# Last row of the output weights loaded and multiplied in two halves of 256 columns

## The chip, the core and the metric

One core of one Trainium2 chip runs the kernel. The metric is the device time of one execution in microseconds (us). The core has TensorE (matmuls and their weight loads), VectorE, ScalarE, GpSimd and SyncE, which work beside one another and wait for each other on semaphores, and 16 DMA engines that move data between the device memory and the on-chip memory. In profile lines they are PE (matmul) and PEld (weight load), DVE, ACT, POOL and SP; SPq and ACTq are DMA issues by SyncE and ScalarE. L38 is line 38 of the kernel, and since TensorE's instructions are written out by a helper there, all of them have that line.

## The reference

One decode step: a normalised row x (512 values) gives queries for 32 heads; each head attends to 8192 cached keys and values of 128; the heads' outputs go through `wo`. A gated unit on the same normalised row gives a gate, and the result is x plus the product of the two. All is float32.

```python
def _A_ref(x, k_cache, v_cache, wq, wo):          # H = 32, Dh = 128, D = 512
    q = (x @ wq) as [B, H, 1, Dh]
    scores = jnp.einsum("bhqd,bhkd->bhqk", q, k_cache) * (Dh ** -0.5)
    p = _softmax(scores, axis=-1)
    o = jnp.einsum("bhqk,bhkd->bhqd", p, v_cache)
    return o as [B, 1, H * Dh] @ wo               # wo: 4096 x 512

def _B_ref(x, w_gate, w_up, w_down):
    return (sigmoid(x @ w_gate) * (x @ w_up)) @ w_down

xn = _layernorm(x)
return x + _A_ref(xn, ...) * _silu(_B_ref(xn, ...))
```

(`_A_ref` and `_B_ref` are abridged here. The kernel takes the gate as the product of the unit's sum with its sigmoid.)

## The kernel before

**Stages.** Queries, gate and up weights come first. Then 16 pairs of heads are worked through (`NP`, the loop at line 440): VectorE multiplies a pair's keys with the query and sums them (`scores`), ScalarE takes the exponents (`powers_of`), TensorE multiplies them with the values (`pair`, 128 records of 512 columns for each pair), and the pair's output is turned into columns of `o_all` (`place`). All large loads are issued by SyncE in program order, each as soon as its slot is free. ScalarE issues the load of x at the start (line 240).

**The gate.** `column_sums` (line 327) puts the 512 sums of the gated unit onto four partitions, 0, 32, 64 and 96, with 128 consecutive columns each, and `g_row` holds sum times sigmoid in that layout (lines 370 to 373 and line 458). `x_row` holds x in the same layout.

**The tail.** `wo` is viewed as 128 partitions with 32 rows of 512 values each, row r of a partition following row r-1 in memory. It comes in nine loads that end at the rows in `W_ENDS` (line 91): rows 0 to 9, 10 to 15, and so on, at last rows 28 and 29 together, row 30 and row 31 (lines 483 to 485). A load of a single row has 128 runs of 2 KB. The first 28 rows (`W_FOLD`) are multiplied with their columns of `o_all` either on VectorE (`W_DVE`, lines 507 to 516) or on TensorE (`W_PE`, lines 521 to 525); `to_fold` adds these into `s_tmp`.

The rows 28 to 31 (`direct`, line 527) go straight into the sum `acc`, on the four partitions of the gate's layout: for each row four matmuls of 128 columns with one column of weights, one for each group of 32 columns of the array (lines 528 to 532). Behind row 30, `fold` adds the 128 partitions of `s_tmp` into the same `acc` with four matmuls whose weights are ones (lines 492 to 498). Row 31 is last. VectorE multiplies `acc` with `g_row` (line 537), adds `x_row` (line 539), and SyncE stores four runs of 512 bytes (line 562). Before that SyncE waits at line 552 for the load of row 30 (`ld_o[-2]`), goes through the branch at the end of the body, and then waits for the sum.

**What sets the order.** Nothing is planned: each engine follows its own program, and waits on semaphore counts. `Later` (line 18) notes TensorE's instructions and plays them in the order in which they were noted; the tail's are those in `after` (line 540).

Of the kernel before, what the change touches and what calls it, by code (L numbers as in the profile page):

```python
# [13 lines left out]
P = 128  # L14
# [37 lines left out]
def kernel(  # L52
# [13 lines left out]
    _, H, S, Dh = k_cache.shape  # L66
    D = x.shape[-1]
# [4 lines left out]
    NP = H // 2  # L72
    NG = 4
    GP = P // NG
    GC = D // NG
# [3 lines left out]
    WR = H * Dh // P  # L79
    WP = Dh // WR  # L80
# [10 lines left out]
    W_ENDS, W_FOLD = (10, 16, 20, 23, 26, 28, 30, 31, 32), 28  # L91
# [1 line left out]
    W_DVE = [r for r in range(W_FOLD) if r not in W_PE]  # L93
    V_CUTS, K_CUTS = (NB // 2, NB * 13 // 16), {NP - 3: (NB * 3 // 4,), NP - 2: (NB * 3 // 4,), NP - 1: (NB // 2,)}

    N_SEMS = 40
    DVE, ACT, SP, POOL = nc.vector, nc.scalar, nc.sync, nc.gpsimd
    PE = Later(nc.tensor)
    pe_only = OrderedEngineSet([nc.tensor.engine])
# [4 lines left out]
    s_out = nc.alloc_semaphore("s_out")  # L104

    def sb(name, *shape):
        return nc.alloc_sbuf_tensor(name, [P, *shape], F32)[:]
# [8 lines left out]

    pick = sb("pick", 2 * HT)
    slots = [sb(f"slot{i}", SLOT) for i in range(3)]
    x_row, g_row = sb("x_row", GC), sb("g_row", GC)
    ones, ident = sb("ones", P), sb("ident", P)  # L120


# [2 lines left out]
    s_tmp, part = q_all[:, :D], [q_all[:, (1 + n) * D:(2 + n) * D] for n in range(2)]  # L125
# [9 lines left out]
    o_all = sb("o_all", WR)  # L135
# [2 lines left out]
    psum = bank("psum", P, NK * QT)  # L138
    banks = [psum[:, i * QT:(i + 1) * QT] for i in range(NK)]
    big, po, wide = banks[:2], banks[2], banks[3:]  # L140
    acc, pt, o_t = wide[0][:, :GC], wide[1][:, :P], wide[2][:GP, :H * WP + Dh]
    pm, pn = wide[3][:, :4], wide[4][:GP, :Dh]


# [15 lines left out]
    pe, dve, act, pool = (Steps(n) for n in ("s_pe", "s_dve", "s_act", "s_pool"))  # L160
    loads = {}

    def load(eng, name, dst, src, *after):
        wait(eng, *after)
        if name not in loads:
            loads[name] = [semaphore(f"s_{name}"), 0]
        loads[name][1] += 16
        ins = eng.dma_start(dst, src)  # L168
        if not tc.compiled:
            tc.no_tile_sem_insts.add(ins.ins.name)  # L170
        ins.then_inc(loads[name][0], 16)
        return loads[name][0], loads[name][1]

    def wait(eng, *steps):
        for s in steps:
            if s is not None:
                eng.wait_ge(*s)
# [3 lines left out]
    maxed, reduced, powers, copied = (semaphore(f"s_{n}") for n in ("maxed", "reduced", "powers", "copied"))  # L181
# [6 lines left out]
    xv = x.rearrange("a b d -> (a b d)")  # L188
# [49 lines left out]

    c_xrow = dve(DVE.memset(x_row, 0.0))
    ld_xr = load(ACT, "xr", x_row[0:P:GP, :], xv.rearrange("(g c) -> g c", g=NG), c_xrow)  # L240
    ACT.nop().then_inc(q_free, NK)
    ACT.nop().then_inc(s_val[1], 16 * (NP - 2))
    ACT.nop().then_inc(s_val[2], 16 * (NP - 1))
# [17 lines left out]
    t = dve(DVE.reduce_sum(st[:, 0:1], x_col, axis=AX.X))  # L261
    wait(PE, t)
    t = pe(PE.matmul(pt[:, 0:1], ones, st[:, 0:1], start=True, stop=True))
    wait(DVE, t)
    t = dve(DVE.tensor_scalar(st[:, 1:2], pt[:, 0:1], 1.0 / D, None, op0=ALU.mult))
    wait(DVE, t)
    t = dve(DVE.tensor_scalar(xc, x_col, st[:, 1:2], None, op0=ALU.subtract))
    wait(DVE, t)
    t = dve(DVE.tensor_mul(sq, xc, xc))
    wait(DVE, t)  # L270
    t = dve(DVE.reduce_sum(st[:, 2:3], sq, axis=AX.X))
    wait(PE, t)
    t = pe(PE.matmul(pm[:, 0:1], ones, st[:, 2:3], start=True, stop=True))
    wait(ACT, t)
    t = act(ACT.activation(st[:, 3:4], pm[:, 0:1], AF.Sqrt, bias=eps_t, scale=1.0 / D))
    wait(DVE, t)
    t = dve(DVE.reciprocal(st[:, 4:5], st[:, 3:4]))
# [16 lines left out]
    for k in range(KT - 1):  # L294
        wait(DVE, ld_wq[k // 2] if k % 2 == 0 else None, t if k else None)
        t = in_place(wq_t, k)
# [5 lines left out]
              start=True, stop=True).then_inc(q_spread, 1)  # L302
    each_q = PE.take()
    for t in range(NQ):
        c = slice(t * QT, (t + 1) * QT)
        y = wq_t[:, 0, c]
# [3 lines left out]
        for e, h in enumerate(HALF):  # L310
            ins = ACT.copy(qb[h, 2 * t:2 * t + 2, :], q[h, :, e, :])
# [14 lines left out]

    def column_sums(dst, src):
        for g in range(NG):
            ins = PE.matmul(dst[g * GP:g * GP + 1, :GC], ones[:, 0:1], src[:, g * GC:(g + 1) * GC], start=True, stop=True)
        return pe(ins)  # L330

    rows = []
# [2 lines left out]
    for dst, src, ld in zip(sums, (wg_t, wu_t), (ld_g, ld_u)):  # L335
        wait(DVE, ld)
        for k in range(KT):
            t = in_place(src, k)
            wait(DVE, t)
        wait(PE, t, None if rows else (q_free, NK))  # L340
        for d, c in zip(dst, chunks):
            ins = PE.matmul(d[:, :c.stop - c.start], ones, src[:, 0, c], start=True, stop=True)
# [3 lines left out]
    for d, c in zip(sums[0], chunks):  # L346
        t = act(ACT.activation(sg[:, c], d[:, :c.stop - c.start], AF.Sigmoid))
    wait(DVE, t, rows[1])
    for d, c in zip(sums[1], chunks):
        t = dve(DVE.tensor_mul(hg[:, c], sg[:, c], d[:, :c.stop - c.start]))  # L350
# [3 lines left out]
    for g in range(NG):  # L354
        r = slice(g * GP, (g + 1) * GP)
        dve(DVE.transpose(hid[r, :FP, :], hg[r, g * FW:(g + 1) * FW].rearrange("p (i c) -> p c i", c=FP)))
    n = FL // NG
    for g in range(NG):
        r = slice(g * GP, (g + 1) * GP)
# [4 lines left out]
    for c in range(FP + FC):  # L364
        g = c % NG * GP
# [38 lines left out]
    summed, turned_out = {}, {}  # L404

    def all_max(i):
        DVE.wait_ge(turned, i + 1)
        DVE.reduce_max(mx[:1, 1:3], pt[0:1, :].rearrange("o (e p) -> o e p", e=2), axis=AX.X).then_inc(reduced, 1)  # L408
# [31 lines left out]
    for i in range(NP):  # L440
        if i > 0:
            all_max(i - 1)
        if i >= 2:
            load_keys(i, pieces(*K_CUTS.get(i, ())), summed[i - 2])
            if i < NP - 1:
                load_values(i - 1, FULL, (valued, i - 1))
        if i == NP - 1:
            for v, cut in ((i - 1, V_HALVES), (i, V_THREE)):
                load_values(v, cut[:1], (halved, v))
                load_values(v, cut[1:], (valued, v))  # L450
        scores(i)
        if i > 0:
            powers_of(i - 1)
            parts(i - 1)
            heads_out(i - 1)
        if i == 1:
            wait(DVE, c_sig)
            c_gate = dve(DVE.tensor_mul(g_row, g_row, big[1][:, :GC]))
    all_max(NP - 1)
    powers_of(NP - 1)  # L460
    wait(DVE, parts(NP - 1))
# [17 lines left out]


    wo_t = slots[NP % 2 ^ 1].rearrange("p (r e) -> p r e", e=D)
    ld_o = []
    for n, (r0, r1) in enumerate(zip((0,) + W_ENDS, W_ENDS)):
        ld_o.append(load(SP, f"wo{n}", wo_t[:, r0:r1, :], wo.rearrange("(p r) e -> p r e", r=WR)[:, r0:r1, :],
                         summed[NP - 2] if n == 0 else None))


    def to_fold(after):
        wait(DVE, after, t_part)
        return dve(DVE.tensor_add(s_tmp, part[0], big[0]))  # L490

    def fold(dst, copied, last):

        wait(PE, copied)
        for g in range(NG):
            ins = PE.matmul(dst[g * GP:g * GP + 1, :GC], ones[:, 0:1], s_tmp[:, g * GC:(g + 1) * GC],
                            start=last, stop=last)
        return ins

    piece = {r: ld for ld, *ends in zip(ld_o, (0,) + W_ENDS, W_ENDS) for r in range(*ends)}  # L500
# [6 lines left out]
    for k, r in enumerate(W_DVE):  # L507
        n = k % 2
# [16 lines left out]
                        start=(k < NG), stop=(k + NG >= len(W_PE)))  # L525
    folded = to_fold(pe(ins))
    direct = list(range(W_FOLD, WR))
    for r in direct:
        landed(PE, r, direct)
        for g in range(NG):  # L530
            ins = PE.matmul(acc[g * GP:g * GP + 1, :], o_all[:, r:r + 1], wo_t[:, r, g * GC:(g + 1) * GC],
                            start=(r == W_FOLD), stop=(r == WR - 1))
        if r == WR - 2:

            fold(acc, folded, False)
    wait(DVE, pe(ins))
    t = dve(DVE.tensor_mul(g_row, g_row, acc))  # L537
    wait(DVE, t)
    t = dve(DVE.tensor_add(g_row, g_row, x_row))  # L539
    after = PE.take()  # L540


# [6 lines left out]
        PE.play(each)  # L549
    PE.play(after)  # L550

    wait(SP, ld_o[-2])
    nc.regs_alu(once, once, 1, op=ALU.add)
    for e in (ACT, DVE, PE.engine, POOL, SP):
        br = e.br_lt(once, 1, on_true="body", on_false="leave")
# [3 lines left out]
    nc.switch_bb("leave")  # L559

    wait(SP, t)
    SP.dma_start(out.rearrange("a b (g c) -> (a b g) c", g=NG), g_row[0:P:GP, :]).then_inc(s_out, 16)


    used = sorted(s.num for s in sems)
# [33 lines left out]
```

## Time and profile before

| what | us |
|---|---|
| median of 3 runs | 684.65 |
| lowest and highest | 684.42, 684.74 |
| profiled execution | 684.69 |
| its span, first to last instruction | 683.3 |
| VectorE busy in it | 616.0 |
| TensorE matmuls busy in it | 218.8 |
| ScalarE busy in it | 44.6 |

The span is what the profile shows; 1.39 us of the profiled execution lie around it. All times in profile lines count from the span's start. A window line gives a stretch, its length, each engine's busy time with the number of instructions in flight, the clock granted to TensorE as a share of full speed, the busy share of the DMA engines, and GB/s. A timeline line gives start, duration, engine, line, operation, output<-inputs, shapes and count, and in brackets the engine's idle time before it and what ended that.

### The profile page before, as it was taken

The page shows a single profiled execution, that of the slowest core. Times are in us where ns is not written, and L with a number is a line of the kernel's source. Part 1 is how long each engine was busy: PE and PEld are TensorE (multiplying, and loading weights), DVE is VectorE, ACT ScalarE, POOL GpSimd, SP SyncE. Part 2 cuts the span into 40 slices and gives each one's busy share as a digit, 9 for nine tenths or more (in the row PEclk, how much of TensorE's full clock was granted, in tenths as well). Part 3 has the DMA queues.
Part 4 walks back from the last instruction along what each step waited for, and adds up shares of the span by engine and source line. Part 5 has one row for each costly group of instructions (what it writes and reads, how often), then busy time and mean ns, then how long its engine had stood idle before and what let it go on. Part 6 is the DMA issues. An engine that isn't in the chain of part 4 may idle for free. (4 is left out here: it accounts for less than half of the span.)

```text
span 683.3 us, 3400 instructions
## 1 busy us (share of the span) xinstructions
PE 218.8 (32%) x1376; PEld 62.3 (9%) x1376; DVE 616.0 (90%) x156; ACT 44.6 (7%) x142; POOL 2.6 (0%) x11
## 2 busy tenths in 40 slices
PE   0363025050503305050512306060512406060665
PEld 0120001010100101010100101010100101010110
DVE  3869999999999999998989899898989999999917
ACT  2040010000000100000010100000010101000010
POOL 0000000000000000000000000000000000000000
PEclk9987557575755757575665757575665757575897
DMA  9999999999999999999999999999999999999997
GB/s 382 429 440 460 437 434 430 430 430 430 430 430 430 430 430 430 460 441 445 434 430 430 430 430 430 430 430 430 430 437 437 460 430 403 472 399 430 435 430 331
DMA packets 7552, 293.67 MB, mean 430 GB/s; under 512 B 856, under 2 KB 864, under 8 KB 1664
## 3 DMA queue, kind: packets, MB, share of 16 engines
q1 hardware_dynamic: 7544, 293.67, 99.5%
q10 hardware_dynamic: 8, 0.00, 0.0%
HBM read 293.67 MB, written 0.00 MB: 430 GB/s over the span
## 5 line engine op out<-in xcount | busy, mean ns | idle before, releaser
L415 DVE TENSOR_TENSOR slot<-slot,q_all 128x16384 f32<-128x16384 f32 (+3 forms) x19 | 275.9, 14520 | 19.9 <-DMA slot<-in_A_k_cache_dram 19.9
L416 DVE TENSOR_REDUCE sc<-slot 128x128 f32<-128x16384 f32 (+3 forms) x19 | 276.0, 14525 | 0.7
L38 PE MATMUL psum<-slot,zeros 128*8 128x512 f32 x1024 | 148.5, 739 | 253.6 <-PEq L38 253.6
L38 PEld LDWEIGHTS psum<-slot,zeros 128*8 128x8 f32 x1024 | 30.3, 103 | 358.2 <-issue 358.2
L38 PE MATMUL psum<-ident,mx 128*1 128x128 f32 x32 | 8.4, 360 | 114.3 <-PEq L38 114.3
L437 ACT COPY o<-psum 128x512 f32<-128x512 f32 x16 | 9.4, 586 | 400.1 <-PE psum L38 400.1
L38 PE MATMUL psum<-slot,ones 128*128 (+3 forms) x36 | 17.7, 668 | 22.1 <-PEq L38 16.6
L290 DVE SCALAR_TENSOR_TENSOR slot<-slot,xn 128x1376 f32<-128x1376 f32 (+1 forms) x8 | 18.9, 2360 | 3.0 <-DMA slot<-in_A_wq_dram 2.7
L38 PE MATMUL psum<-o,pick 128*2 128x128 f32 x128 | 16.5, 272 | 12.8 <-PEq L38 12.8
L423 DVE STREAM_TRANSPOSE psum<-psum 32x128 f32<-32x128 f32 x16 | 5.0, 310 | 11.1 <-PE psum L38 11.1
L428 ACT ACTIVATE nb<-psum 128x2 f32<-128x2 f32 x16 | 2.8, 172 | 156.1 <-PE psum L38 156.1
L430 ACT ACTIVATE zeros<-sc,nb 64x128 f32<-64x128 f32 x32 | 12.8, 399 | 0.9
L38 PEld LDWEIGHTS psum<-ident,mx 128*1 128x1 f32 x32 | 1.8, 80 | 118.4 <-issue 118.3
L38 PEld LDWEIGHTS psum<-o,pick 128*2 128x2 f32 x128 | 9.9, 84 | 29.6 <-issue 27.2
L38 PE MATMUL psum<-slot,o_all 128*1 128x128 f32 (+1 forms) x54 | 9.5, 463 | 6.5 <-DMA slot<-in_A_wo_dram 6.5
L38 PE MATMUL psum<-zeros,rs 128*32 128x2 f32 x32 | 3.7, 187 | 23.5 <-PEq L38 23.5
L408 DVE TENSOR_REDUCE mx<-psum 1x2 f32<-1x128 f32 x16 | 4.4, 277 | 7.5 <-PE psum L38 7.5
L38 PE MATMUL psum<-mx,ones 1*128 1x2 f32 x32 | 8.2, 324 | 7.4 <-PEq L38 7.4
L515 DVE SCALAR_TENSOR_TENSOR q_all<-slot,o_all,q_all 128x512 f32<-128x512 f32 x15 | 10.0, 747 | 0.0
L38 PEld LDWEIGHTS psum<-slot,ones 128*128 128x128 f32 (+1 forms) x36 | 7.0, 218 | 32.5 <-issue 24.7
L38 PE MATMUL psum<-slot,o 128*1 128x512 f32 x26 | 5.0, 827 | 11.2 <-DMA slot<-in_B_w_down_dram 11.2
L38 PEld LDWEIGHTS psum<-mx,ones 1*128 1x128 f32 x32 | 7.3, 282 | 14.0 <-issue 14.0
(54 smaller groups left out, 61.3 us busy)
## 6 DMA issues: line engine op xcount, KB each, us to landing
slot<-in_A_k_cache_dram SPq DMA_DIRECT2D x2, 6144.0 KB, 37.9
slot<-in_A_v_cache_dram SPq DMA_DIRECT2D x3, 4096.0 KB, 23.0
slot<-in_A_wq_dram SPq DMA_DIRECT2D x2, 4096.0 KB, 16.6
slot<-in_A_k_cache_dram SPq DMA_DIRECT2D x2, 4096.0 KB, 40.5
slot<-in_A_k_cache_dram SPq DMA_DIRECT2D x2, 2048.0 KB, 42.4
slot<-in_B_w_gate_dram SPq DMA_DIRECT2D x1, 2752.0 KB, 26.9
slot<-in_B_w_up_dram SPq DMA_DIRECT2D x1, 2752.0 KB, 33.0
slot<-in_B_w_down_dram SPq DMA_DIRECT2D x1, 2560.0 KB, 22.7
```

The costliest lines, as they stand in the source:

```text
L38: ins = getattr(self.engine, name)(*args, **kwargs)
L290: return dve(DVE.scalar_tensor_tensor(y, w[:, k, cols], xn[:, k:k + 1], y, op0=ALU.mult, op1=ALU.add))
L408: DVE.reduce_max(mx[:1, 1:3], pt[0:1, :].rearrange("o (e p) -> o e p", e=2), axis=AX.X).then_inc(reduced, 1)
L415: wait(DVE, dve(DVE.tensor_mul(k[:, j, :], k[:, j, :], qb[:, i:i + 1, :].to_broadcast([P, n, Dh]))))
L416: summed[i] = dve(DVE.reduce_sum(sc[i % 2][:, j], k[:, j, :], axis=AX.X))
L423: turned_out[i] = dve(DVE.transpose(o, pn.rearrange("e (a r) -> e a r", r=WR)))
L428: wait(ACT, act(ACT.mul(nb, pm[:, :2], -SCALE)))
L430: ACT.activation(weights[h, :, e * HT:(e + 1) * HT], sc[i % 2][h].rearrange("p (g b) -> p g b", b=HT), AF.Exp, bias=nb[h, e:e + 1], scale= ...
L437: ACT.copy(o1, po).then_inc(copied, 1)
L515: ins = DVE.scalar_tensor_tensor(part[n], wo_t[:, r, :], col, part[n], op0=ALU.mult, op1=ALU.add)
```

## The change

The last row of `wo`, row 31, is loaded as two loads of 256 columns each (128 runs of 1 KB), so there are ten `wo` loads. The sum `acc` becomes two PSUM tiles of 64 columns in two banks, one for each half of the 512 columns; all matmuls that add into it, those of rows 28 to 30 and the fold too, are issued as eight of 64 columns instead of four of 128. When the first half of row 31 has landed, its four matmuls run and VectorE multiplies its 64 columns with the gate; then the same for the second half. One sum with x follows over all 128 columns.

The layout on the four partitions changes with it: each holds 64 columns of the first half and 64 of the second. So `column_sums` reads its operand with a stride, the store has eight runs of 256 bytes, and x is loaded a second time in the new layout into a new tile `x_add`, which is cleared at the start; ScalarE issues that load in the loop's second round, after the copy for pair 0. `x_row` stays for the normalisation. `N_SEMS` grows by two, and SyncE's wait before the branch names the load of row 30 as before, now `ld_o[-3]`.

```diff
-    x_row, g_row = sb("x_row", GC), sb("g_row", GC)
+    x_row, g_row, x_add = sb("x_row", GC), sb("g_row", GC), sb("x_add", GC)
...
-    acc, pt, o_t = wide[0][:, :GC], wide[1][:, :P], wide[2][:GP, :H * WP + Dh]
+    pt, o_t = wide[1][:, :P], wide[2][:GP, :H * WP + Dh]
+    acc = [wide[n][:, :GC // 2] for n in range(2)]
...
+    c_xadd = dve(DVE.memset(x_add, 0.0))
...
     def column_sums(dst, src):
         for g in range(NG):
-            ins = PE.matmul(dst[g * GP:g * GP + 1, :GC], ones[:, 0:1], src[:, g * GC:(g + 1) * GC], start=True, stop=True)
+            ins = PE.matmul(dst[g * GP:g * GP + 1, :GC].rearrange("r (h c) -> r h c", h=2), ones[:, 0:1],
+                            src.rearrange("p (h g c) -> p g h c", h=2, g=NG)[:, g], start=True, stop=True)
...
         if i == 1:
             wait(DVE, c_sig)
             c_gate = dve(DVE.tensor_mul(g_row, g_row, big[1][:, :GC]))
+            ld_xa = load(ACT, "xa", x_add[0:P:GP, :].rearrange("g (h c) -> g h c", h=2),
+                         xv.rearrange("(h g c) -> g h c", h=2, g=NG), c_xadd)
...
-    ld_o = []
+    ld_o, halves = [], (slice(0, D // 2), slice(D // 2, D))
     for n, (r0, r1) in enumerate(zip((0,) + W_ENDS, W_ENDS)):
-        ld_o.append(load(SP, f"wo{n}", wo_t[:, r0:r1, :], wo.rearrange("(p r) e -> p r e", r=WR)[:, r0:r1, :],
-                         summed[NP - 2] if n == 0 else None))
+        for c in halves if r1 == WR else (slice(0, D),):
+            ld_o.append(load(SP, f"wo{n}_{c.start}", wo_t[:, r0:r1, c], wo.rearrange("(p r) e -> p r e", r=WR)[:, r0:r1, c],
+                             summed[NP - 2] if n == 0 else None))
...
-    def fold(dst, copied, last):
-
-        wait(PE, copied)
+    def into_groups(n, col, row, **flags):
         for g in range(NG):
-            ins = PE.matmul(dst[g * GP:g * GP + 1, :GC], ones[:, 0:1], s_tmp[:, g * GC:(g + 1) * GC],
-                            start=last, stop=last)
+            c = slice(halves[n].start + g * GC // 2, halves[n].start + (g + 1) * GC // 2)
+            ins = PE.matmul(acc[n][g * GP:g * GP + 1, :], col, row[:, c], **flags)
         return ins
...
-    for r in direct:
+    for r in direct[:-1]:
         landed(PE, r, direct)
-        for g in range(NG):
-            ins = PE.matmul(acc[g * GP:g * GP + 1, :], o_all[:, r:r + 1], wo_t[:, r, g * GC:(g + 1) * GC],
-                            start=(r == W_FOLD), stop=(r == WR - 1))
-        if r == WR - 2:
-
-            fold(acc, folded, False)
-    wait(DVE, pe(ins))
-    t = dve(DVE.tensor_mul(g_row, g_row, acc))
-    wait(DVE, t)
-    t = dve(DVE.tensor_add(g_row, g_row, x_row))
+        for n in range(2):
+            into_groups(n, o_all[:, r:r + 1], wo_t[:, r, :], start=(r == W_FOLD), stop=False)
+    wait(PE, folded)
+    for n in range(2):
+        into_groups(n, ones[:, 0:1], s_tmp, start=False, stop=False)
+    wait(DVE, ld_xa)
+    for n, ld in enumerate(ld_o[-2:]):
+        wait(PE, ld)
+        ins = into_groups(n, o_all[:, WR - 1:], wo_t[:, WR - 1, :], start=False, stop=True)
+        wait(DVE, pe(ins))
+        y = g_row[:, n * GC // 2:(n + 1) * GC // 2]
+        t = dve(DVE.tensor_mul(y, y, acc[n]))
+    wait(DVE, t)
+    t = dve(DVE.tensor_add(g_row, g_row, x_add))
...
-    wait(SP, ld_o[-2])
+    wait(SP, ld_o[-3])
...
-    SP.dma_start(out.rearrange("a b (g c) -> (a b g) c", g=NG), g_row[0:P:GP, :]).then_inc(s_out, 16)
+    SP.dma_start(out.rearrange("a b (h g c) -> (a b g) h c", h=2, g=NG),
+                 g_row[0:P:GP, :].rearrange("g (h c) -> g h c", h=2)).then_inc(s_out, 16)
```

## Rows read from the trace of the kernel before

**Rows 1.** The page, parts 1 and 2: busy time by engine; DMA by slice.
```profile
PE 218.8 (32%) x1376; PEld 62.3 (9%) x1376; DVE 616.0 (90%) x156; ACT 44.6 (7%) x142; POOL 2.6 (0%) x11
...
DMA  9999999999999999999999999999999999999997
```

**Rows 2.** The chain that ended last: start us, us, what.
```profile
650.58 28.68 DMA slot<-in_A_wo_dram
...
679.29 1.23 PE psum L38 x32
...
680.54 0.44 PE psum L38 x8
```

**Rows 3.** The timeline of the tail, all engines.
```profile
647.73 10.98 SPq L168 DMA_DIRECT2D slot<-in_A_wo_dram  x9
...
679.90 0.11 PEld L38 LDWEIGHTS psum<-slot,o_all 128*1 128x1 f32 x8 [0.29 <-DMA slot<-in_A_wo_dram]
...
680.12 0.40 PE L38 MATMUL psum<-q_all,ones 128*1 128x128 f32 x8
680.54 0.11 PEld L38 LDWEIGHTS psum<-slot,o_all 128*1 128x1 f32 x8 [0.31 <-DMA slot<-in_A_wo_dram]
...
681.00 0.29 DVE L537 TENSOR_TENSOR g_row<-g_row,psum 128x128 f32<-128x128 f32 x1 [1.19 <-PE psum L38]
...
681.65 0.63 SPq L562 DMA_DIRECT2D out_dram<-g_row  x1
```

**Rows 4.** Waits of SyncE: us in total, times, longest.
```profile
SPq L553 <- DMA slot<-in_A_wo_dram: 21.2, 1, 21.2
```

**Rows 5.** TensorE's groups by shape: busy us, mean ns, idle before, releasers.
```profile
L38 PE MATMUL psum<-slot,o_all 128*1 128x128 f32 x32 | 1.4, 271 | 0.2 <-DMA slot<-in_A_wo_dram 0.2
...
L38 PEld LDWEIGHTS psum<-slot,o_all 128*1 128x1 f32 x54 | 1.1, 81 | 14.9 <-DMA slot<-in_A_wo_dram 12.3 <-issue 2.6
```

**Rows 6.** Windows of 0.02 us, TensorE alone: length, busy (in flight), clock, DMA, GB/s.
```profile
679.28:679.30 0.02, 0.01 (x1) 1.00 0.79 307
679.30:679.32 0.02, 0.02 (x4) 1.00 0.58 205
...
679.40:679.42 0.02, 0.02 (x7) 1.00 2.16 820
```

**Rows 7.** The timeline of TensorE's weight loads while one pair's values are multiplied.
```profile
605.36 0.16 PEld L38 LDWEIGHTS psum<-slot,zeros 128*8 128x8 f32 x4 [0.69 <-issue]
...
608.50 0.10 PEld L38 LDWEIGHTS psum<-slot,zeros 128*8 128x8 f32 x4 [0.33 <-issue]
```

**Rows 8.** VectorE's groups by shape: the two smallest products on PSUM.
```profile
L469 DVE TENSOR_TENSOR psum<-psum,den 32x96 f32<-32x96 f32 x1 | 0.3, 252 | 0.0
...
L469 DVE TENSOR_TENSOR psum<-psum,den 32x32 f32<-32x32 f32 x1 | 0.2, 187 | 0.0
```

**Rows 9.** DMA of the cache stream, 60 to 600 us.
```profile
DMA packets 4369, 235.10 MB, mean 435 GB/s; under 512 B 496, under 2 KB 496, under 8 KB 528
```

**Rows 10.** Windows, all engines in the page's order, clock, DMA share, GB/s.
```profile
605.00:606.00 1.00, 1.00 (x8) 0.16 (x4) 1.00 (x1) 0.00 (x0) 0.00 (x0) 0.50 1.14 492
...
608.00:609.00 1.00, 1.00 (x16) 0.28 (x12) 0.97 (x2) 0.00 (x0) 0.00 (x0) 1.00 0.99 426
...
678.00:679.00 1.00, 0.95 (x4) 0.09 (x4) 0.47 (x1) 0.00 (x0) 0.00 (x0) 1.00 1.00 399
```

**Rows 11.** Issues of `wo` loads: duration ns, min/median/max.
```profile
L168 SPq DMA_DIRECT2D slot<-in_A_wo_dram x9: 430/432/4160, 647.7 to 655.3; - x9
```

**Rows 12.** The timeline of the start, VectorE's and ScalarE's first steps.
```profile
2.18 0.17 DVE L239 MEMSET x_row<- 128x128 f32 x1 [2.18 <-PEq L196]
...
2.38 1.08 ACTq L168 DMA_DIRECT2D x_row<-in_A_x_dram  x1
...
9.10 0.40 DVE L260 STREAM_TRANSPOSE g_row<-x_row 128x128 f32<-128x128 f32 x1 [6.75 <-DMA x_row<-in_A_x_dram]
```

More of the change, by code (lines that the diff above doesn't have):

```diff
@@ L94 @@
     V_CUTS, K_CUTS = (NB // 2, NB * 13 // 16), {NP - 3: (NB * 3 // 4,), NP - 2: (NB * 3 // 4,), NP - 1: (NB // 2,)}
-    N_SEMS = 40
+    N_SEMS = 42
     DVE, ACT, SP, POOL = nc.vector, nc.scalar, nc.sync, nc.gpsimd
```

## The prediction

> **What bounds the kernel now.** I read the utilisation lines of the page first. Over the whole span the DMA engines are nearly always busy, while VectorE is at 90% and TensorE at 32%; only the last slice falls off [rows 1]. So the time is that of one long load, and what lies behind its last bytes. An edit of a few small operations can act on the end only, after the load stream has run dry, or nowhere.
>
> The chain of waits says what that end is: loads of `wo` up to 679.26 (650.58 + 28.68), then TensorE to 680.98 (680.54 + 0.44) [rows 2], and behind it on VectorE the product with the gate, the sum with x, and the store. The timeline resolves it. Rows 28 and 29 of `wo` start at 679.29 [rows 2], row 30 at 679.90 after a DMA wait, the fold (which needs no load) right behind it, row 31 at 680.54 after another DMA wait [rows 3]. The spacing 679.29, 679.90, 680.54 is 0.61 and 0.64 us for 256 KB each. The fold's eight records begin at 680.12 [rows 3] and run in two sets 0.107 us apart (next part), so TensorE could have begun row 31 near 680.34; it waited some 0.2 us more for the load. Row 31 is therefore the one with the load on the path, and behind it stand: 0.46 us from its first matmul to VectorE's start (680.54 to 681.00), two VectorE operations (the product 0.29 us, the sum much the same, done before 681.65), and 0.63 us of issue by SyncE at 681.65 [rows 3]. The rest up to the span's end at 683.3 is the store's completion. All told 683.3 - 680.54 = 2.8 us follow the landing; more than that this edit can't remove.
>
> **How these matmuls run.** One float32 matmul shows as two records (rows 28 to 31 are 16 instructions and 32 records [rows 5]). In windows of 0.02 us the records in flight are 1 from 679.28, 4 from 679.30 and 7 from 679.40 [rows 6]: four start almost together, on the four column groups, and the next four about 0.107 us later (an estimate; the fold's 0.40 us [rows 3] is one such step more than a record's 0.27 to 0.29 us [rows 5]). The granted clock there is 1.00, the level of 2.4 GHz [rows 6]. The longer matmuls do likewise: for 512 columns four weight loads come every 0.33 + 0.10 = 0.43 us near 608.5 and every 0.69 + 0.16 = 0.85 us near 605.4 [rows 7], where the granted clock was 1.00 and 0.50, 2.4 and 1.2 GHz [rows 10]. 0.43 / 0.107 = 4, the ratio of the columns. So the time of a set of four has so far followed columns alone.
>
> **The change, part by part.**
> **Matmuls of rows 28 to 30 and of the fold.** 16 instructions of 128 columns become 32 of 64: 16 sets of four records instead of 8. By columns a set costs 0.107 / 2 = 0.053 us, and the total is unchanged. If a set costs 0.107 us whatever its columns, the total doubles, and TensorE is late. No row has a set of 64 columns in such a run. I take 0.053 us, since the rows with 512 and 128 columns agree with proportion [rows 6, 7], and keep 0.107 us for the range. At 0.053 us the fold ends near 680.34 as now, still covered by the wait for the last load.
>
> **Row 31 in two halves.** The first half should land some 0.3 us ahead of the second (half of 0.64 us), near 680.27. Its matmuls go behind the fold, 680.34 to 680.45, its VectorE product at about 680.69 to 680.91. Cover: the second half's load and matmuls; were that gone, 0.22 us would come back. On the path stands the second half alone: two sets of 64 columns instead of two of 128. The second set starts 0.053 us earlier behind the first, and its records are shorter by another 0.054 us: -0.107 us. Its product with the gate has 64 columns instead of 128. VectorE's small operations on PSUM took 252 ns at 96 columns and 187 ns at 32 [rows 8], so 1.0 ns per column: -0.065 us. The sum with x stays whole at 0.29 us.
>
> **The load itself.** The same 256 KB, in 256 runs of 1 KB instead of 128 of 2 KB, and a second completion. Free, if bytes count alone; +0.60 us, if a packet of 1 KB takes as long as one of 2 KB (eight more packets on each of 16 engines, each 2 KB at 435 / 16 = 27 GB/s, 75 ns). Nearest rows: the cache stream moved 235.1 MB in 4369 packets, over 50 KB each, at 435 GB/s [rows 9], and the last pieces of `wo`, runs of a few KB, 399 GB/s from 678 to 679 [rows 10]. 2 KB on one of 16 engines takes 75 ns at 435 and 82 ns at 399 GB/s, so some 7 ns hang on the packet; nine more (eight of data and a completion) give +0.06 us. I take 0.05.
>
> **Extra issue on SyncE.** One more `wo` issue, 0.43 us, some of which were held back (the longest took 4.16 us [rows 11], all were out by 647.73 + 10.98 = 658.7 [rows 3]). Held back the same way, a tenth is out by about 662.5, far ahead of the 680 at which its data move; SyncE then only waits, 21.2 us, for row 30 [rows 4]. At nothing; cover is that wait.
>
> **Second copy of x.** A memset (0.17 us like the one of `x_row`) falls into VectorE's 6.75 us of waiting for x at the start. ScalarE issues a 2 KB load after pair 0's copy; the first such issue took 1.08 us [rows 12], and behind it on ScalarE stand the exponents of the next pair. ScalarE is busy 7% of the time [rows 1] and the load stream does not wait for it. At nothing; without cover 1.1 us once. VectorE's late wait for it is met 600 us before. The gate's sums with a strided operand (four matmuls of 128 columns, as the fold, 0.40 us [rows 3]) run once, under the load stream: nothing, at most 0.4 us.
>
> **The store.** Eight runs of 256 bytes for four of 512. Bounds 0 and +0.63 us, a whole second issue. A `wo` issue with 128 runs took 0.43 us [rows 11], less than this one with four, so the number of runs does not set it: 0.
>
> **Sum.** -0.107 - 0.065 + 0.05 = -0.12 us. The profiled execution took 684.69 us (span 683.3 and 1.39 us around it), 0.04 us over the median of 684.65. Against its own time that is 684.57, against the median 684.53: I say 684.55.
>
> **The rivals.**
> **TensorE becomes the bound of the tail.** From 679.29 to the second half stand 18 sets (8 of rows 28 and 29, 4 of row 30, 4 of the fold, 2 of the first half). At 0.107 us per set the second half starts at 679.29 + 18 x 0.107 = 681.22, VectorE's product 0.107 + 0.30 us later, at 681.62 instead of 681.00: +0.62 - 0.065 = +0.56 us, 685.2. It ties with today at 0.078 us a set. For it: nothing shows a set faster than 0.107 us, and weight loads of a single column record 81 ns each [rows 5]. Against: four start within 0.04 us [rows 6]. The Trainium skill (TensorE: Matmul & The Clock Gate, section "Wait — 56ns, not 53.3ns?") says that matmuls never start less than about 25 ns apart, however few columns; that would be 0.1 us for four and this rival's result, some 685.1. Starts within one set disagree with it here, since four records are in flight 0.04 us after the first window.
>
> **1 KB packets at the price of 2 KB.** +0.60 - 0.17 = +0.43 us, 685.1. Against it: packets shrink from over 50 KB to a few KB and the rate falls by 8% only [rows 9, 10].
>
> **Slower: the instructions can't be supplied.** The tail from 679.29 has 40 pairs of weight load and matmul now, and 80 then, without a long wait between. Pairs queued while TensorE waited come at 0.027 us (four per 0.107), but the longest such run without a wait is 16 pairs. The fastest long run is that of the 512-column matmuls, a pair per 0.107 us [rows 7]; if 40 more pairs cost that, +4.3 us, 688.9. It decides from (1.37 + 0.12) / 40 = 0.037 us per further pair on. Against: that run is explained by its columns, so it doesn't show a limit of supply. The same page and section says that the sequencer, where it decodes in microcode, spends about 62 ns per matmul and binds once the array's work is shorter; an estimate by it is 40 x 0.062 = +2.5 us, 687.1. No run here shows a stretch long enough to tell.
>
> **The change does nothing.** If both halves land together, the first half's product is late and takes back 0.22 us: 684.8.
>
> **How the numbers follow.** What a measurement can tell from no change is 0.2%, 1.37 us here. Forecast 0.62; TensorE bound 0.20; dear packets 0.10; supply 0.05; halves together 0.03. All but the supply lie within 0.2%, and only some way not seen, which would have to remove half of what follows the last landing, makes it faster by that: 0.01, taken from "halves together". Faster 0.01, same 0.94, slower 0.05. The range goes from 684.2 (free packets, 684.48, less the 0.23 us that the lowest run lies below the median) to 685.3 (TensorE bound, 685.2, and a little of the same spread); it leaves out the supply alone and the edges.
>
> **What would show it.** After: the load of the second half ends near 680.58; two sets of 64 columns behind it; VectorE's second product starts near 680.93 and takes 0.22 us; SyncE's store near 681.5. If the weight loads of rows 28 to 30 come back to back up to 681, with no DMA wait ahead of the last set, TensorE is the bound. If the DMA wait ahead of the second half grows by tenths of a us, packets are dear. If there are gaps between sets with nothing waited for, it is the supply. A store that takes longer from issue to the end than 1.65 us (681.65 to 683.3) contradicts my price of nothing for it. The prediction is wrong if any stretch before 679 has moved by more than a few tenths of a us.

## The result, and the profile after

The change made the kernel slower: 686.86 us (median of 16 runs, 685.49 to 688.6) against 685.04 us for the kernel before in the same comparison (16 runs, 684.42 to 685.78). The ratio is 1.0028, with an interval from 1.0021 to 1.0034, so +0.28% or some 1.8 us. The forecast was 684.55 us, with a range up to 685.3: a small gain in the tail and nothing anywhere else.

The tail behaves nearly as forecast. This is the timeline of the changed kernel's end, as in [rows 3] (start us, duration us, engine, line, operation, and in brackets the idle time before and what ended it):

```profile
680.49 0.44 PEld L38 LDWEIGHTS psum<-slot,o_all 128*1 128x1 f32 x32 [1.12 <-DMA slot<-in_A_wo_dram]
...
681.12 0.22 PEld L38 LDWEIGHTS psum<-slot,o_all 128*1 128x1 f32 x16 [0.19 <-DMA slot<-in_A_wo_dram]
...
681.51 0.16 PEld L38 LDWEIGHTS psum<-slot,o_all 128*1 128x1 f32 x8
681.57 0.57 PE L38 MATMUL psum<-slot,o_all 128*1 128x64 f32 x16
681.85 0.11 PEld L38 LDWEIGHTS psum<-slot,o_all 128*1 128x1 f32 x8 [0.17 <-DMA slot<-in_A_wo_dram]
682.00 0.43 DVE L545 TENSOR_TENSOR g_row<-g_row,psum 128x64 f32<-128x64 f32 x2 [0.96 <-PE psum L38]
682.46 0.29 DVE L547 TENSOR_TENSOR g_row<-g_row,x_add 128x128 f32<-128x128 f32 x1
...
682.78 0.67 SPq L570 DMA_DIRECT2D out_dram<-g_row  x1
```

The weight loads stop for the second half of row 31 (the wait of 0.17 us at 681.85), as they stopped for the whole of row 31 before [rows 3]. From the start of rows 28 and 29 to the end of the span it is 684.5 - 680.49 = 4.01 us; before it was 683.3 - 679.29 = 4.01 us. So the tail has gained nothing and lost nothing. But it starts 1.20 us later: 680.49 instead of 679.29 [rows 2]. The time was lost before the tail began.

The page's DMA queues (packets, MB, share of 16 engines' span) show one thing that is new. First the kernel before, then the changed one:

```profile
q1 hardware_dynamic: 7544, 293.67, 99.5%
q10 hardware_dynamic: 8, 0.00, 0.0%
```

```profile
q1 hardware_dynamic: 7692, 293.67, 99.4%
q8 instruction: 1, 0.02, 0.0%
q10 hardware_dynamic: 20, 0.00, 0.0%
```

The bytes of the data are the same. The further packets on q1 are the split row (144) and the store (4), those on q10 the second load of x. On q8, which the kernel before doesn't have, stands one packet of instructions, 0.02 MB. The DMA view of the changed kernel from 106 to 108 us shows when it ran, on the same engines as the cache loads:

```profile
DMA packets 17, 1.06 MB, mean 532 GB/s; under 512 B 0, under 2 KB 0, under 8 KB 0
q1 hardware_dynamic: 16, 1.05, 122.5%
q8 instruction: 1, 0.02, 2.9%
```

2.9% of 16 engines in 2 us is 0.029 x 16 x 2 = 0.93 us of one engine. (That q1 stands at 122.5% says that the view's shares are rough in so short a window.) The next rows are one key load of the kernel before: SyncE's issue on the timeline (start us), then the DMA issues (last number: us from issue to landing).

```profile
92.13 0.33 SPq L168 DMA_DIRECT2D slot<-in_A_k_cache_dram  x1
```

```profile
slot<-in_A_k_cache_dram SPq DMA_DIRECT2D x1, 27.6
```

The same two rows of the changed kernel:

```profile
90.10 0.33 SPq L169 DMA_DIRECT2D slot<-in_A_k_cache_dram  x1
```

```profile
slot<-in_A_k_cache_dram SPq DMA_DIRECT2D x1, 30.8
```

Before, the load lands at 92.13 + 27.6 = 119.7 us; after, at 90.10 + 30.8 = 120.9 us, 1.2 us later although it was issued earlier. The same sum for other loads of keys and values in the two kernels:

| lands before, us | lands after, us | later by |
|---|---|---|
| 81.0 | 80.9 | -0.1 |
| 100.3 | 100.2 | -0.1 |
| 119.7 | 120.9 | 1.2 |
| 139.0 | 140.2 | 1.2 |
| 196.9 | 198.1 | 1.2 |
| 525.4 | 526.6 | 1.2 |
| 602.7 | 604.0 | 1.3 |

The whole delay of the profiled execution arises between 100.3 and 119.7 us and is carried to the end by a load stream that has no slack [rows 1]. The profiled execution took 685.89 us (span 684.5 and 1.39 us around it, as before); that accounts for 1.2 of the 1.8 us of the medians. The other 0.6 us lies in runs longer than the profiled one and is taken up below.

### The profile page after: what moved, and what is told of

Read it like the earlier page. It is cut to its first block, busy times and chain, and to the rows that moved or that the text cites. A ratio compares the mean times of both kernels' runs of the same rounds, so it can differ in the third digit from the quotient of the medians.

```text
span 684.5 us, 3485 instructions
## 1 busy us (share of the span) xinstructions
PE 219.5 (32%) x1416; PEld 62.3 (9%) x1416; DVE 615.9 (90%) x158; ACT 44.6 (7%) x142; POOL 2.6 (0%) x11
## 3 DMA queue, kind: packets, MB, share of 16 engines
q1 hardware_dynamic: 7692, 293.67, 99.4%
## 5 line engine op out<-in xcount | busy, mean ns | idle before, releaser
L38 PE MATMUL psum<-slot,ones 128*128 (+3 forms) x36 | 15.8, 609 | 21.9 <-PEq L38 16.5
L38 PE MATMUL psum<-slot,o_all 128*1 128x64 f32 (+1 forms) x86 | 11.1, 385 | 5.1 <-DMA slot<-in_A_wo_dram 5.1
```

The costliest lines, as they stand in the source:

```text
L38: ins = getattr(self.engine, name)(*args, **kwargs)
```

## The experiments

Each ran beside the kernel before (medians of it in the three comparisons: 685.0, 684.9 and 685.06 us). "Slip" is how much later than before the key load of 119.7 us lands, from landings rounded to 0.1 us.

### First comparison: which part of the change costs it?

Candidates were the second load of x, whose issue on ScalarE lies near 109 us, the split of row 31 or the store, and the fetch of instructions, if it belongs to the longer program.

**The load of x moved to the start.**

```
...
     c_xadd = dve(DVE.memset(x_add, 0.0))
+    ld_xa = load(ACT, "xa", x_add[0:P:GP, :].rearrange("g (h c) -> g h c", h=2),
+                 xv.rearrange("(h g c) -> g h c", h=2, g=NG), c_xadd)
...
         if i == 1:
...
-            ld_xa = load(ACT, "xa", x_add[0:P:GP, :].rearrange("g (h c) -> g h c", h=2),
-                         xv.rearrange("(h g c) -> g h c", h=2, g=NG), c_xadd)
```

> The changed kernel, but x_add is loaded by ScalarE at the start, right behind x_row. Theory A (the small load in the middle of the cache stream costs the stream 1.2 us or more, and the tail costs nothing): every cache load lands within 0.2 us of the kernel before, ratio to before 0.9995 to 1.0005, a profiled end near 683.3. Rival B (the split last row or the eight-run store costs the time): still 1.8 us slower, ratio about 1.0026. If both share it, something between, about +0.6 us, 1.0009.

Measured: 686.14 us, ratio 1.0020 (1.0011 to 1.0029), slip 1.0 us, one q8 packet. The load is gone from the middle of the stream and the slip stays.

**Only the load of x, in the kernel before**; `x_add` enters no result, and VectorE's wait stands ahead of its product with the gate. (The tile and one semaphore for it are left out of the lines below.)

```
...
+    c_xadd = dve(DVE.memset(x_add, 0.0))
...
         if i == 1:
...
+            ld_xa = load(ACT, "xa", x_add[0:P:GP, :].rearrange("g (h c) -> g h c", h=2),
+                         xv.rearrange("(h g c) -> g h c", h=2, g=NG), c_xadd)
...
+    wait(DVE, ld_xa)
```

> The kernel before, plus only the clearing of x_add and its load by ScalarE in the second round; nothing reads the tile. Theory A: the cache loads from about 120 us on land 1.2 us later, ratio about 1.0018 to 1.0028. Rival B: nothing moves, ratio 1.0000 within 0.0005. If the instruction fetch seen beside it (16 KB near 106 us) carries the slip and belongs to the longer program of the changed kernel, there is no fetch here and no slip.

Measured: 685.03 us, ratio 1.0000 (0.9991 to 1.0009), slip -0.1 us. The page's queues of this kernel:

```profile
q1 hardware_dynamic: 7544, 293.67, 99.4%
q10 hardware_dynamic: 20, 0.00, 0.0%
```

The 20 packets of q10 are there and the time is that of before: the small load costs nothing, and the first suspicion falls. What is missing is q8.

**Row 31 loaded whole, the matmuls still in halves.**

```
...
-        for c in halves if r1 == WR else (slice(0, D),):
+        for c in (slice(0, D),):
...
-    for n, ld in enumerate(ld_o[-2:]):
+    for n, ld in enumerate((ld_o[-1], None)):
...
```

> The changed kernel with row 31 loaded whole (one load, 2 KB runs) and both halves of the matmuls and products behind that one load; the load of x_add stays in the second round. Theory A: as the changed kernel, about 1.8 us slower than before, ratio 1.0026, with the slip of 1.2 us at 100 to 120 us; the tail 0.1 to 0.3 us longer than the changed kernel's or the same. Rival B (1 KB runs and a second load cost the time): back to the time before, 1.0000.

Measured: 686.83 us, ratio 1.0027 (1.0017 to 1.0037), slip 0.8 us, one q8 packet. The split of the load isn't the cause.

**The load of x issued by SyncE.**

```
-            ld_xa = load(ACT, "xa", x_add[0:P:GP, :].rearrange("g (h c) -> g h c", h=2),
+            ld_xa = load(SP, "xa", x_add[0:P:GP, :].rearrange("g (h c) -> g h c", h=2),
```

> The changed kernel, but x_add is loaded by SyncE, on the queue of the cache loads, behind the first load of values (near 69 us). Theory A in the form that a second queue in the middle of the stream is what costs (its packets between 64 KB packets): no slip, ratio 1.0000 to 1.0006. Theory A in the form that eight runs of 256 bytes cost wherever they stand in the stream: a slip of about 1.2 us, now between the loads that land at 81 and 100 us, ratio 1.0018 to 1.0028. Rival B: 1.0026 with no slip in the stream.

Measured: 686.1 us, ratio 1.0025 (1.0014 to 1.0036), slip 1.1 us, one q8 packet. The queue of that load doesn't matter.

What the three slow kernels share, and the fast one lacks, is the new layout with its store of eight runs, and TensorE's longer program (116 float32 matmuls for 96) with the q8 packet. The next comparison keeps the two apart. By the page, TensorE has 1416 matmul records instead of 1376 [rows 1], and as many weight loads: 20 matmuls are 40 and 40 more.

### Second comparison: is it the length of TensorE's program?

**20, 10 and 90 matmuls added to the kernel before**, of 64 columns each, into a bank that nothing reads, ahead of the tail (the number in `range` is 20, 10 or 90). They change no load, no wait and no other engine.

```
+    for k in range(20):
+        g = k % NG * GP
+        PE.matmul(wide[4][g:g + 1, :GC // 2], ones[:, 0:1], ones[:, :GC // 2], start=True, stop=True)
```

> The kernel before plus 20 matmuls of 64 columns of ones into an unused PSUM bank, issued ahead of the tail's first matmul, where TensorE waits some 2 us for the first rows of wo; TensorE's program then is as long as the changed kernel's (116 float32 matmuls in place of 96), and nothing else changes. Theory F (the changed kernel is slower since its longer TensorE program needs one more fetch of 16 KB of instructions, in the middle of the cache stream, near 106 us): the page shows one packet on the instruction queue, the cache loads from 120 us on land about 1.1 us later, ratio 1.0015 to 1.0028. Rival B (the tail, the store or the layout of the changed kernel cost the time): ratio 1.0000 within 0.0006, no fetch.

Measured with 20: 686.63 us, ratio 1.0028 (1.0019 to 1.0037), slip 1.0 us, the ratio of the whole change to the fourth digit. The queues:

```profile
q1 hardware_dynamic: 7544, 293.67, 99.3%
q8 instruction: 1, 0.02, 0.0%
q10 hardware_dynamic: 8, 0.00, 0.0%
```

The key load of this kernel, as above, lands at 90.19 + 30.5 = 120.7 us:

```profile
90.19 0.33 SPq L168 DMA_DIRECT2D slot<-in_A_k_cache_dram  x1
```

```profile
slot<-in_A_k_cache_dram SPq DMA_DIRECT2D x1, 30.5
```

All data packets are those of before; only q8 is new. So 20 matmuls that do nothing cost what the change costs, and the load at 119.7 us is late some 550 us before they run (at 666.6 us).

> As the kernel with 20 more matmuls, but with 10 (106 in all). Theory F with a limit between 107 and 116 matmuls: no fetch and no slip, ratio 1.0000 within 0.0006. If the time grows with each matmul more instead, half of what 20 cost, about 0.6 to 0.9 us, ratio about 1.0011.

Measured with 10: 687.07 us (5 runs), ratio 1.0035 (1.0022 to 1.0049), slip 1.1 us, one q8 packet at 106 us. Expected had been none: the limit lies below 106 matmuls. A second packet at 686 us lies behind the span's end, and what lies around the span is 2.13 us in the median run instead of 1.37; so its ratio holds more than the slip. The spans alone, 684.9 us in the median against 683.5, are 1.4 us apart.

> As the kernel with 20 more matmuls, but with 90 (186 in all, some 280 instructions more than with 20, so more than another 16 KB). Theory F: two or more packets on the instruction queue, and about double the slip, 2.2 us or more, ratio 1.003 to 1.006, of which up to 0.3 us may come from the matmuls themselves at the start of the tail. Rival: one packet and the slip of the 20.

Measured with 90: 686.61 us (7 runs), ratio 1.0028 (1.0017 to 1.0039). The page's queue of instructions, and the same line of the DMA view from 672 to 674 us:

```profile
q8 instruction: 2, 0.03, 0.0%
```

```profile
q8 instruction: 1, 0.02, 3.0%
```

There are two packets, as expected, but the second is fetched only at 672 us, and the time is not higher than with 20: slip 1.3 us, not twice 1.1. A doubled cost was expected and didn't come. The second fetch has only the end of the `wo` loads behind it; that a fetch costs only where many loads follow it is argued, and no run moves the first packet by itself. The 90 matmuls themselves, on the timeline, show whether a long row of them can be supplied:

```profile
668.40 2.74 PE L38 MATMUL psum<-ones 128*1 128x64 f32 x180 [0.88 <-DVE o_all L472]
```

180 records in 2.74 us are 15 ns each (30 ns a float32 matmul, which is two records), each with a weight load of its own, in one line without a gap.

**Nine matmuls fewer in the changed kernel**, out of the gate's last product (left out: most of the terms of that product).

```
-    for c in range(FP + FC):
+    for c in range(NG):
...
-                        start=(c < NG), stop=(c + NG >= FP + FC))
+                        start=True, stop=True)
```

> The changed kernel with 9 of the 13 matmuls of the gated unit's last product left out (those of w_down's chunks 4 to 12, so the gate is not the reference's), all else as changed: TensorE's program has 107 matmuls in place of 116. These nine run at about 62 us under the load stream, so by themselves they cost nothing. Theory F: no instruction fetch, no slip of the cache loads, ratio 0.9995 to 1.0004: what the change does to the tail is then seen by itself. Rival B: still 1.2 to 1.8 us slower, ratio 1.0018 to 1.0027.

Measured: 686.46 us, ratio 1.0021 (1.0012 to 1.0030), slip 1.1 us, one q8 packet. Expected had been no packet. 107 matmuls are still above the limit, as 106 are; this run and the one with 10 more agree.

### Third comparison: the limit, a program longer by other means, and the spread

**The whole new tail with a program as short as before**: 19 of the gate's matmuls are left out (most terms of its products and sums), 97 remain.

```
-        for g in range(NG):
+        for g in range(1):
...
-        for d, c in zip(dst, chunks):
+        for d, c in zip(dst, chunks[:1]):
...
-    for d, c in zip(sums[0], chunks):
+    for d, c in zip(sums[0][:1] * 3, chunks):
...
-    for c in range(FP + FC):
+    for c in range(1):
```

> The changed kernel with 19 matmuls of the gated unit left out (its gate and up products in two thirds of the columns, 12 of 13 of the last product's, 3 of 4 column sums; the gate is not the reference's), so that TensorE's program has 97 matmuls, one more than the kernel before. All of them ran under the load stream before 70 us. Theory F (the slip is the instruction fetch of a longer TensorE program): no packet on the instruction queue, no slip of the cache loads, and what is left is the change's own effect on the tail: ratio 0.9993 to 1.0005. Rival B (tail, store, layout): 1.0018 to 1.0028.

Measured: 684.69 us, ratio 0.9995 (0.9986 to 1.0004), slip -0.3 us. The page's queues, and its timeline's end:

```profile
q1 hardware_dynamic: 7692, 293.67, 99.5%
q10 hardware_dynamic: 20, 0.00, 0.0%
```

```profile
679.58 0.44 PEld L38 LDWEIGHTS psum<-slot,o_all 128*1 128x1 f32 x32 [1.14 <-DMA slot<-in_A_wo_dram]
...
681.80 0.67 SPq L570 DMA_DIRECT2D out_dram<-g_row  x1
```

All of the change's data packets are here (7692 and 20), no q8, and no loss. The tail takes 683.5 - 679.58 = 3.92 us against 4.01; 0.37 us lie between the medians, which the interval doesn't tell from nothing.

**40 instructions that only wait**, for counts reached long before, in the kernel before (two waits go into one instruction: the page counts 3440 instructions for 3400); no matmul more.

```
+    for k in range(80):
+        PE.wait_ge(pe.sem, 1)
```

> The kernel before plus 40 instructions on TensorE that only wait for counts reached long ago, ahead of the tail's first matmul, where TensorE waits for wo anyway: about as many instructions more as 10 float32 matmuls bring, but no matmul more. Theory F (the number of instructions counts): one instruction fetch near 106 us, slip of about 1.1 us, ratio 1.0015 to 1.0035. Rival (more matmuls, by activity or clock): 1.0000 within 0.0006.

Measured: 687.44 us, ratio 1.0028 (1.0019 to 1.0037), slip 1.0 us. The page's busy line and queues, then the queue of instructions in the DMA view from 104 to 106 us:

```profile
PE 219.4 (32%) x1376; PEld 62.0 (9%) x1376; DVE 615.3 (90%) x156; ACT 44.5 (6%) x142; POOL 2.6 (0%) x11
...
q1 hardware_dynamic: 7544, 293.67, 99.3%
q8 instruction: 1, 0.02, 0.0%
q10 hardware_dynamic: 8, 0.00, 0.0%
```

```profile
q8 instruction: 1, 0.02, 2.9%
```

1376 matmul records as before, and yet the packet, the slip and the loss. It is the number of TensorE's instructions, not what they compute. Part of the median's 2.4 us lies outside the span here too: a second packet stands behind the span's end, between 686 and 688 us, and the spans alone (685.0 us in the median against 683.7) are 1.3 us apart.

**Nine value matmuls of 32 fewer in each pair**, in the changed kernel and in the one before (left out: those terms of the values' sums). TensorE is done sooner with each pair, but 107 matmuls keep the fetch in the changed one. (A pair's 32 matmuls are 64 records, not 128 as said above: the page of the kernel before has 1024 of them for 16 pairs.)

```
+        if V_CUTS[0] < j < V_CUTS[1]:
+            continue
```

> The changed kernel with 9 of the 32 matmuls of each pair's values left out, those of the second half of the values up to the last cut (the attention's output is not the reference's); 107 matmuls in TensorE's program, so the fetch stays. SyncE issues the last values and the first wo load once the matmuls of pair 14 are done; with 7 in place of 16 in that half this comes 1.9 us earlier at full clock, 3.8 us at half. Theory L (what some runs lose beyond the slip of 1.1 us is that this issue comes too late for the queue, by TensorE's clock in that stretch): spans 684.2 to 684.8, all runs within 0.8 us, median about 1.2 us over before, ratio 1.0013 to 1.0019. Otherwise a spread of 2 to 3 us as the changed kernel has, median 1.6 to 2.0 us over before.

Measured, on the changed kernel: 686.13 us (685.69 to 686.98), ratio 1.0018 (1.0009 to 1.0027), slip 1.2 us, one q8 packet.

> The kernel before with the same 9 matmuls left out (87 in the program, no fetch expected): the control for the run of the changed kernel with shorter values. Theory F and L: spans as the fastest of before, 683.0 to 683.6, ratio 0.9993 to 1.0000.

Measured, on the kernel before: 685.0 us, ratio 0.9999 (0.9990 to 1.0008), slip -0.3 us, no q8. So the shorter pairs gain nothing by themselves, but in the changed kernel they take 0.73 us of the 1.8 (+1.07 remain, about the slip), and the runs lie within 1.3 us instead of 3.1 (0.8 was expected).

That answers in part where the 0.6 us beyond the slip come from. The last value pieces and the first load of `wo` are issued by SyncE when pair 14's matmuls are done. Issue of the last values (before, after, the changed kernel with shorter pairs):

```profile
646.88 0.80 SPq L227 DMA_DIRECT2D slot<-in_A_v_cache_dram  x2
```

```profile
648.21 0.80 SPq L228 DMA_DIRECT2D slot<-in_A_v_cache_dram  x2
```

```profile
644.71 0.80 SPq L228 DMA_DIRECT2D slot<-in_A_v_cache_dram  x2
```

And the stretch behind it, as windows (length, VectorE's busy time, granted clock, DMA share, GB/s): before, after, and the kernel with 90 matmuls, whose profiled span of 686.2 us is one of the long ones:

```profile
648.00:656.00 8.00, 3.12 (x9) 0.79 0.99 425
```

```profile
648.00:656.00 8.00, 4.86 (x9) 0.87 0.98 419
```

```profile
648.00:656.00 8.00, 4.36 (x9) 0.98 0.95 369
```

The profiled run of the changed kernel is one of its short ones (span 684.5 us, median 685.5) and moves nearly as much here as before. The long one falls behind: (425 - 369) x 8 us is 0.45 MB, an estimated 1.0 us at 435 GB/s [rows 9]. The two other profiles with spans above 685 us, those with 10 matmuls and with the waits, show 404 and 398 GB/s in this window, and all the shorter ones 416 to 453. So in the profiles this stretch is where the long runs lose more. With the shorter pairs the spread is less than half; they bring the issue forward, but they also change what TensorE does, and no run moves the issue alone. How a late DMA engine would bring this loss about, and why in some runs only, is open.

## Why the prediction was wrong

**The step that failed** is the price of the further matmuls: "By columns a set costs 0.107 / 2 = 0.053 us, and the total is unchanged". It priced 16 instructions becoming 32 by their time on TensorE's array, and had no term for them as instructions that have to be brought in. With it failed the sentence that kept all else at nothing, that an edit of a few small operations "can act on the end only, after the load stream has run dry, or nowhere". The missing term is 1.2 us of slip in the profile; the other 0.6 us of the median come in kernels with the packet only (median spans of 684.7 to 685.5 us, without it 683.3 to 683.7). Here is the chain as the runs show it:

- 116 float32 matmuls instead of 96 are 80 more instructions (a weight load and a matmul record, each twice). Counted in the programs, at four per matmul and about 38 others, TensorE has 422 before and 502 after, an estimate.
- One fetch more appears between the estimated 426 (97 matmuls, no packet) and 461 (106 matmuls, packet), and a second by 781 (186 matmuls; by the page's counts 10 matmuls are 39 instructions more and 90 are 359).
- It comes at 104 to 108 us, while TensorE multiplies the first pair's values, not when it reaches the new code at 680 us, and takes one of 16 DMA engines for 0.93 us in the middle of the cache stream.
- Every load of the stream that was followed lands later from then on, by 0.8 to 1.5 us over the kernels with the packet; in those without it they land between 0.4 us earlier and 0.4 us later.
- At the stream's end one engine is still behind. In windows of 0.4 us (length, TensorE's busy time, clock, DMA share, GB/s) the kernel before runs dry at once:

```profile
679.60:680.00 0.40, 0.40 (x16) 1.00 0.63 241
680.00:680.40 0.40, 0.40 (x16) 1.00 0.05 15
680.40:680.80 0.40, 0.39 (x15) 1.00 0.00 0
```

With 20 more matmuls most engines are done at about the same time, and a share of 0.07, about one engine of 16, goes on for over 1 us (26 GB/s; a sixteenth of 435 is 27):

```profile
679.60:680.00 0.40, 0.40 (x6) 0.56 0.87 333
680.00:680.40 0.40, 0.40 (x8) 1.00 0.11 41
680.40:680.80 0.40, 0.40 (x18) 1.00 0.07 26
680.80:681.20 0.40, 0.40 (x16) 1.00 0.07 26
```

The new tail shows the same pair: without the packet (97 matmuls) the share falls from 0.79 to 0.04 and 0 in the windows from 680.0 us on, with it (the changed kernel) from 0.68 to 0.19, 0.11 and 0.04. TensorE's wait for the last half ends at 681.85 all the same. So a load is complete only with its latest engine, and one engine is about as late at the end as the packet made it. Why the slip ranges from 0.8 to 1.5 us around the packet's 0.93 isn't shown.

The Trainium skill (Runtime: NRT & Kernel Launch, section "Instruction fetch mechanics") states that engines refill their instruction memory in blocks of 16 KiB, 256 instructions, by DMA of their own, at a cost that is mostly hidden. The size agrees with the packet of 0.02 MB, and a second packet between 502 and 781 instructions agrees with 256 further ones; "mostly hidden" doesn't hold here, where the first such block delays the stream by 0.8 to 1.5 us in a kernel that the DMA engines bound; the second one, near the end, costs nothing that shows.

**The supply rival** was given 0.05. Its price from the rows was 688.9 us. By the figure of the Trainium skill (TensorE: Matmul & The Clock Gate, section "Wait — 56ns, not 53.3ns?") it was an estimated 687.1 us, which lies near the result. But its mechanism, gaps between instructions in the tail, fell. It would have needed over 0.037 us per pair; 180 pairs came at 0.015 us. That 687.1 lies close is luck.

**The prediction's own warning** fits: it named as wrong "any stretch before 679 [that] has moved by more than a few tenths of a us". The stretch from 107 us on has, by 1.2 us. What it lacked was a candidate for how a tail could act there. It priced the steps added before the tail "at nothing", each for a reason of its own, and missed that the instructions of the tail share a program with all that runs before.

**The tail, term by term.**
- Sets of 64 columns: row 30 and the fold, 32 records or eight sets, run from 681.12 to 681.57, 0.056 us a set against 0.053 forecast. The rival with 0.107 us a set falls. The floor of some 25 ns between starts that the Trainium skill gives (TensorE: Matmul & The Clock Gate, section "Wait — 56ns, not 53.3ns?") disagrees with this row if each record counts as a start: on four column groups it is 0.056 / 4 = 14 ns a record. A float32 matmul, which is two records, takes 28 ns.
- The second half, from its matmuls' start to the end of its product: 682.43 - 681.85 = 0.58 us. Before it was 0.75 (680.54 to 681.29), and with the 0.17 forecast for matmul and product it was to be 0.58. The two products of 64 columns take 0.43 us together, 0.22 each as forecast.
- The first half came in time, with nothing to spare. Its matmuls follow the fold without a wait for a load (681.51), 0.3 us ahead of the second half's, so the two didn't land together, and the rival "the change does nothing" falls. VectorE starts its product at 682.00 and goes straight into the second one; the forecast, too, left only 0.02 us between them (680.91 and 680.93).
- The load of row 31: from the start of rows 28 and 29 to the last half's matmuls 681.85 - 680.49 = 1.36 us, before 680.54 - 679.29 = 1.25 us. That is +0.11 us where 0.05 was taken; with the row loaded whole (the third kernel of the first comparison) the same stretch took 1.27 us. The dear packets of the rival, +0.60 us, fall.
- The store: 684.5 - 682.78 = 1.72 us against 1.65, +0.07 where 0 was taken, 0.04 of it in its issue (0.67 against 0.63).
- Sum: -0.17 for matmul and product, as forecast; the costs of +0.11 and +0.07 take it all back, 4.01 us before and after. One profile can't tell a tenth of a us, though: the kernels with the old tail take 4.01 to 4.12 us from the start of rows 28 and 29 to the end, and the new tail without the packet takes 3.92, which is 0.09 less where 0.12 was forecast.

**Further steps.** The second copy of x is free, as forecast (1.0000 with it alone). The issues of `wo` run longer than forecast and still cost nothing where they lie (the changed kernel's timeline, and SyncE's waits):

```profile
649.06 16.21 SPq L169 DMA_DIRECT2D slot<-in_A_wo_dram  x10
```

```profile
SPq L561 <- DMA slot<-in_A_wo_dram: 15.8, 1, 15.8
```

They are out at 665.3 us instead of the forecast 662.5, and SyncE's wait for row 30 shrinks from 21.2 [rows 4] to 15.8 us. That wait was the cover, and it has held.

## What to carry to other kernels

Count an engine's instructions before and after an edit, not only their time: in this kernel, which the DMA engines bound, one further block of TensorE's instructions cost one to two microseconds although the new code stood at the very end, and the page shows it as a packet on the instruction queue. Where a small edit of the end costs more than the end can explain, compare when the same load lands in both kernels, from the start on; the first one that differs tells where to look. And test the cause with dead instructions of the same number, since a change that is split by its parts alone leaves what the parts share unseen.

## What the runs showed of the hardware

- A fetch of 16 KB of instructions (0.02 MB on the page) took 0.93 us of one DMA engine (2.9% of 16 engines in 2 us), shifted the loads behind it by 0.8 to 1.5 us, and was made at 104 to 108 us, though the instructions that were added run at 666 us and later.
- With the packet, about one DMA engine (a share of 0.07) was still at work over 1 us after the others at the end of the loads, and the wait for the last load ended only with it (in the changed kernel at 681.85, with the share below 0.2 since 680.4).
- Instructions that only wait count towards it as matmuls do: 40 of them brought the packet and moved the kernel from 685.06 to 687.44 us (ratio 1.0028), 1.3 us of it within the span.
- Float32 matmuls of 64 columns on four column groups ran at 14 to 15 ns a record, with as many weight loads beside them, over 180 records in a row.
